# One inversion for both softmax sums, a gate product ahead of the fifth weight product, and later q/k loads, in an attention-plus-GLU kernel

## The chip, the cores and the metric

The kernel runs on one core of a Trainium2 chip. The metric is the device time of one execution in microseconds (us); an execution of this kernel takes about 829 us. The trace gives the *span*, from the first to the last instruction; it is some 1.7 to 2.2 us shorter than the time.

## The reference

For each of 4 batches (6016 rows, 256 columns) q and k are normalised by column and make a 256x256 matrix that passes through a softmax. v times that matrix goes into a gated unit.

```python
def _attn_ref(q, k, v, tau):
    qn = q / (np.linalg.norm(q, axis=1, keepdims=True) + 1e-06)
    kn = k / (np.linalg.norm(k, axis=1, keepdims=True) + 1e-06)
    s = kn.transpose(0, 2, 1) @ qn / tau
    s = s - s.max(-1, keepdims=True)
    a = np.exp(s)
    a /= a.sum(-1, keepdims=True) + 1e-09
    return (v @ a).astype(np.float32)

def _moe_ref(x, w_gate, w_val, w_out):
    gate = 1.0 / (1.0 + np.exp(-(x @ w_gate)))
    val = x @ w_val
    return (gate * val @ w_out).astype(np.float32)
```

## The kernel before

The kernel never forms v times the attention matrix. It multiplies the 256x256 matrix into the two weight matrices, G for the gate and H for the value (12 products per batch: three column groups, two matrices, two row halves), and then works on v directly. A *slot* is one step of the main loop: a gate pair of matmuls (`ps_gate`), a value pair (`ps_val`), the sigmoid on ScalarE, their product `hT` on VectorE, and four output matmuls (`ps_o`) of the chunk before. Twelve slots make a chunk of 512 rows. The next batch's loads, squares and scores are hung on slots as side work.

```python
def sums(b, i, pl=psm, tag="m"):          # one row half
    ps_r = pl.tile([P, 1], FP32, tag=tag, name="ps_r")
    for j in range(CB):
        mm(ps_r, s["e"][i][:, j, :], ones_bf[:, 0:1], j == 0, j == CB - 1)
    r = attp.tile([P, 1], FP32, tag=f"rrow{i}", name="rrow", bufs=2)
    invert(r, ps_r, 1e-9, 1.0)            # one add, one reciprocal on VectorE
# sums_both: the same for both halves in one PSUM tile, used by batches 1 to 3
# gh(b, n, pool, tag, act): product n into PSUM, then scaled by rrow and stored
# in bf16 by ScalarE (act) or VectorE
...
# batch 0, before the main loop
sums(0, 0)
gh(0, 0, psg, "g", act=False)
sums(0, 1, pss, "s")
gh(0, 1, psg, "g", act=True)
gh(0, 2, psv, "v", act=False)
gh(0, 3, psv, "v", act=True)
nc.scalar.preload_act_table(ACT.Sigmoid)
gh(0, 4, pso, "o", act=False)
...
# side work of batch b, for batch n = b + 1
at(ci * FC + 2, transpose_v, nb, nci)     # DMA transpose, SyncE's queue
at(ci * FC + 0, load_v, lb, lci)          # four v buffers, GpSimd's queue
first, last = (14 if b == 0 else 0), 8 * FC
for g, (t0, nt) in enumerate(groups):     # 12 groups of q and k
    s0 = first + g * (last - first) // NCH
    at(max(0, s0 - 20), load_qk, n, t0, nt)
...
# main loop
glu(b, ci, f)
flush()                                   # copies ps_o; the output store, SyncE's queue
if prev is not None and not block:
    out_mms(*prev, f * TPC, (f + 1) * TPC)
for fn, a in side.get((ci, f), ()):
    fn(*a)
if (b, ci) == (0, 0) and f < len(gh_order) - 5:
    gh(0, 5 + f, pso, "o")                # two PSUM tiles
```

## Time and profile before

| kernel before | value |
|---|---|
| median of three runs | 829.21 us (829.09, 829.21, 829.82) |
| the execution that the trace was taken in | 830.27 us, span 828.2 us |
| TensorE (PE) busy | 807.9 us, 98% |
| VectorE, ScalarE busy | 71%, 47% |

In this page PE is the bound; an idle PE costs its full length, and idleness elsewhere costs nothing. Useful here are PE's list of waits, the timeline with the time that an engine was idle before an instruction in square brackets, and the DMA issues with their time to landing. The traced execution was 1.06 us slower than the median.

### The profile page before, as it was taken

The numbers are of one execution on the slowest core, as the hardware profiler recorded it, in microseconds if no ns is written. First come the engines' busy times: TensorE is split into PE (matmuls) and PEld (weight loads), VectorE is DVE, ScalarE is ACT, GpSimd is POOL, SyncE is SP. The second block draws the span as 40 slices with busy tenths as digits, with TensorE's granted clock in tenths as the row PEclk, the third lists the DMA queues.
The fourth block names the chain that finished last, engine by engine and source line by source line (L and its number), as shares of the span: only waits on it lengthen the run. The fifth ranks groups of instructions, "written<-read, shape, count | busy, mean of one in ns | idle before, by whom it ended". The sixth has DMA issues, their size and how long they took to land.

```text
span 828.2 us, 13621 instructions
## 1 busy us (share of the span) xinstructions
PE 807.9 (98%) x5122; PEld 499.1 (60%) x5134; DVE 590.2 (71%) x1025; ACT 392.2 (47%) x644; POOL 78.9 (10%) x151
## 2 busy tenths in 40 slices
PE   4799999999999999999999999999999999999998
PEld 2456666665665666665576666666566566666666
DVE  5777777887667777778767777777766666666665
ACT  3754444446644444445654444444655444444442
POOL 4432100002201100000221010000000000000000
PEclk9999999999999999999999999999999999999999
DMA  9999823226746443223875452223322323322211
GB/s 214 206 200 195 126 52 89 55 58 133 158 85 124 96 85 60 57 51 83 157 141 123 81 108 60 51 60 78 64 58 63 75 52 84 61 58 68 47 36 71
DMA packets 77874, 77.17 MB, mean 93 GB/s; under 512 B 50672, under 2 KB 55792, under 8 KB 77808
## 3 DMA queue, kind: packets, MB, share of 16 engines
q0 software_dynamic: 22768, 38.81, 28.5%
q1 hardware_dynamic: 54752, 36.91, 17.6%
q8 instruction: 40, 0.66, 0.3%
q10 hardware_dynamic: 288, 0.59, 0.2%
q14 instruction: 26, 0.21, 0.1%
HBM read 78.64 MB, written 24.64 MB: 125 GB/s over the span
## 4 chain that ended last, share of the span: by engine, by line
PE 92%; DMA 6%; DVE 1%; issue 0%; POOL 0%; ACT 0%; POOLq 0%
PE ps_o L88 29%; PE ps_gate L88 29%; PE ps_val L88 29%; PE ps_s L88 4%; DMA k_sb<-in_k_dram 3%; PE ps_gh L88 2%; DMA vT<-v_sb 2%; DMA w_gate<-in_moe_w_gate_dram 1%; DVE hT L434 0%; DVE sq L184 0%; PE ps_end L88 0%; ACT g_sb L433 0%; POOL q_sb L98 0%; PE ps_n L88 0%; POOL k_sb L98 0%
## 5 line engine op out<-in xcount | busy, mean ns | idle before, releaser
L434 DVE TENSOR_TENSOR hT<-ps_val,g_sb 128x512 bf16<-128x512 f32 (+1 forms) x576 | 391.0, 679 | 205.7 <-ACT g_sb L433 200.8
L433 ACT ACTIVATE g_sb<-ps_gate 128x512 bf16<-128x512 f32 (+1 forms) x576 | 338.2, 588 | 386.8 <-PE ps_gate L88 380.5
L88 PE MATMUL ps_gate<-vT,gh_G 128*128 128x512 bf16 (+1 forms) x1152 | 337.5, 375 | 0.7 <-DMA vT<-v_sb 0.5
L88 PE MATMUL ps_val<-vT,gh_H 128*128 128x512 bf16 (+1 forms) x1152 | 337.5, 375 | 0.3
L88 PE MATMUL ps_o<-w_out_sb,hT 128*128 128x256 bf16 x2244 | 324.9, 273 | 0.0
L88 PEld LDWEIGHTS <-hT 128*128 128x128 bf16 x2268 | 221.0, 98 | 124.7
L88 PEld LDWEIGHTS <-gh_H 128*128 128x128 bf16 x1152 | 112.7, 98 | 131.7 <-issue 1.0
L88 PEld LDWEIGHTS <-gh_G 128*128 128x128 bf16 x1152 | 112.4, 98 | 38.3 <-DMA vT<-v_sb 0.8
L460 DVE COPY out_sb<-ps_o 128x256 f32<-128x256 f32 x187 | 77.4, 414 | 12.6 <-PE ps_o L88 12.6
L88 PE MATMUL ps_s<-k_sb,q_sb 128*128 128x256 bf16 x376 | 71.2, 293 | 14.6 <-DMA k_sb<-in_k_dram 7.6
L108 POOL DMA_DIRECT2D v_sb<-in_v_dram x48 | 25.5, 532 | 601.3 <-DMA vT<-v_sb 452.0
L88 PEld LDWEIGHTS <-q_sb 128*128 128x128 bf16 x376 | 39.2, 105 | 23.7 <-issue 9.6
L223 DVE TENSOR_TENSOR acc<-acc,sq 128x1024 bf16<-128x1024 bf16 (+1 forms) x66 | 44.2, 669 | 0.0
L184 DVE TENSOR_TENSOR sq<-q_sb 128x1024 bf16<-128x1024 bf16 (+2 forms) x42 | 28.0, 666 | 1.2 <-DMA q_sb<-in_q_dram 1.1
L98 POOL DMA_DIRECT2D q_sb<-in_q_dram x44 | 24.2, 549 | 38.5 <-PE ps_s L88 12.4
L98 POOL DMA_DIRECT2D k_sb<-in_k_dram x44 | 24.0, 544 | 14.5 <-DMA k_sb<-in_k_dram 7.7
L184 DVE TENSOR_TENSOR sq<-k_sb 128x1024 bf16<-128x1024 bf16 (+2 forms) x34 | 22.4, 658 | 0.2 <-DMA k_sb<-in_k_dram 0.2
L182 ACT ACTIVATE sq<-k_sb 128x1024 bf16<-128x1024 bf16 (+1 forms) x11 | 10.7, 1010 | 12.0 <-DMA k_sb<-in_k_dram 8.9
L88 PEld LDWEIGHTS <-e_sb 128*128 128x128 bf16 x112 | 10.2, 98 | 6.0 <-issue 1.0
L88 PE MATMUL ps_gh<-w_val,e_sb 128*128 128x512 bf16 x45 | 13.5, 379 | 0.2
L88 PE MATMUL ps_gh<-w_gate,e_sb 128*128 128x512 bf16 x41 | 12.7, 379 | 1.0 <-DMA w_gate<-in_moe_w_gate_dram 0.8
L433 ACT ACT_TABLE_LOAD x6 | 7.7, 1283 | 9.0 <-PE ps_gate L88 9.0
(69 smaller groups left out, 123.2 us busy)
## 6 DMA issues: line engine op xcount, KB each, us to landing
out_dram<-out_sb SPq DMA_DIRECT2D x44, 512.0 KB, 2.9
v_sb<-in_v_dram POOLq DMA_DIRECT2D x44, 256.0 KB, 3.9
q_sb<-in_q_dram POOLq DMA_DIRECT2D x35, 256.0 KB, 6.5
k_sb<-in_k_dram POOLq DMA_DIRECT2D x35, 256.0 KB, 7.7
q_sb<-in_q_dram POOLq DMA_DIRECT2D x4, 512.0 KB, 11.5
k_sb<-in_k_dram POOLq DMA_DIRECT2D x4, 512.0 KB, 13.4
out_dram<-out_sb SPq DMA_DIRECT2D x3, 384.0 KB, 3.0
w_gate<-in_moe_w_gate_dram POOLq DMA_DIRECT2D x3, 256.0 KB, 8.0
```

What stands on the lines that cost most here:

```text
L88: nc.tensor.matmul(out, lhsT=lhsT, rhs=rhs, start=start, stop=stop, **kw)
L98: nc.gpsimd.dma_start(out=tl[:, :nt, :], in_=rows(src, b)[:, t0 : t0 + nt, :])
L108: nc.gpsimd.dma_start(out=v_sb[:, :nt, :], in_=rows(v, b)[:, t0 : t0 + nt, :])
L182: nc.scalar.activation(out=sq[:, :nt, :], in_=src[:, :nt, :], func=ACT.Square)
L184: engine.tensor_tensor(out=sq[:, :nt, :], in0=src[:, :nt, :], in1=src[:, :nt, :], op=ALU.mult)
L223: nc.vector.tensor_tensor(out=acc[:, :nt, :], in0=acc[:, :nt, :], in1=st[b]["sq", w][:, :nt, :], op=ALU.add)
L433: nc.scalar.activation(out=g_sb[:, :n], in_=ps_gate[:, :n], func=ACT.Sigmoid)
L434: nc.vector.tensor_tensor(out=hts[b, ci][:, f, :n], in0=ps_val[:, :n], in1=g_sb[:, :n], op=ALU.mult)
L460: nc.vector.tensor_copy(out=out_sb[:, s, :], in_=ps)
```

## The change

Its intent: fewer VectorE steps between the sums and the first stores; the gate pair in place of a wait for weights; and q/k loads of the second batch that no longer crowd what is needed sooner.

```diff
-    sums(0, 0)
-    gh(0, 0, psg, "g", act=False)
-    sums(0, 1, pss, "s")
+    ps_first = gh_mms(0, 0, psg, "g")
+    sums_both(0)
+    gh_store(0, 0, ps_first, False)
     gh(0, 1, psg, "g", act=True)
     gh(0, 2, psv, "v", act=False)
     gh(0, 3, psv, "v", act=True)
     nc.scalar.preload_act_table(ACT.Sigmoid)
-    gh(0, 4, pso, "o", act=False)
...
-            half = nt * CB // 2
-            (nc.scalar.copy if late is None else late)(vT[:, half : nt * CB, :], ...)
+            half = nt * CB // 2 if late else nt * CB
+            if late:
+                late(vT[:, half : nt * CB, :], ...)
...
-            at(max(0, s0 - 20), load_qk, n, t0, nt)
+            at(max(0, s0 - (12 if b == 0 else 20)), load_qk, n, t0, nt)
...
+    gh_first = {f: (5 + f,) for f in range(len(gh_order) - 7)}
+    gh_first[len(gh_order) - 7] = tuple(range(len(gh_order) - 2, len(gh_order)))
...
-                glu(b, ci, f)
+                glu(b, ci, f, (lambda: gh(0, 4, pso, "o", act=False)) if first else None)
...
-                if (b, ci) == (0, 0) and f < len(gh_order) - 5:
-                    gh(0, 5 + f, pso, "o")
+                if (b, ci) == (0, 0):
+                    for i in gh_first.get(f, ()):
+                        gh(0, i, pso, "o")
```

`glu` calls its new argument between the gate pair and the value pair. The second transposed v tile now leaves PSUM through VectorE alone, and the last two products share slot 5.

More of the change, by code (lines that the diff above doesn't have):

```diff
@@ L336, in exps @@
         s.setdefault("rrow", [])
-    def sums(b, i, pl=psm, tag="m"):
-        s = st[b]
-        ps_r = pl.tile([P, 1], FP32, tag=tag, name="ps_r")
-        for j in range(CB):
-            mm(ps_r, s["e"][i][:, j, :], ones_bf[:, 0:1], j == 0, j == CB - 1)
-        r = attp.tile([P, 1], FP32, tag=f"rrow{i}", name="rrow", bufs=2)
-        invert(r, ps_r, 1e-9, 1.0)
-        s["rrow"].append(r)
     def sums_both(b):
@@ L370, with gh_mms @@
     gh_order = [(fg, w, i) for fg in range(NFG) for w in range(2) for i in range(CB)]
-    def gh(b, n, pl=None, tag=None, act=None):
+    def gh_mms(b, n, pl, tag):
         s = st[b]
         fg, w, i = gh_order[n]
-        ps = (pl or psm).tile([P, FG], FP32, tag=tag or "m", name="ps_gh")
+        ps = pl.tile([P, FG], FP32, tag=tag, name="ps_gh")
         for j in range(CB):
@@ L383, in gh, with gh_store @@
             )
+        return ps
+    def gh_store(b, n, ps, act):
+        s = st[b]
+        fg, w, i = gh_order[n]
         dst = s["gh"][w][fg][:, i, :]
         r = s["rrow"][i]
-        if act if act is not None else n % 2 == 0:
+        if act:
             nc.scalar.activation(out=dst, in_=ps, func=ACT.Copy, scale=r)
@@ L389, in gh @@
             nc.vector.tensor_scalar(out=dst, in0=ps, scalar1=r, scalar2=None, op0=ALU.mult)
+    def gh(b, n, pl, tag, act=None):
+        gh_store(b, n, gh_mms(b, n, pl, tag), n % 2 == 0 if act is None else act)
     vts = {}
@@ L406, in transpose_v @@
                 )
-            half = nt * CB // 2
-            (nc.scalar.copy if late is None else late)(vT[:, half : nt * CB, :], ps[:, half : nt * CB, :])
+            half = nt * CB // 2 if late else nt * CB
+            if late:
+                late(vT[:, half : nt * CB, :], ps[:, half : nt * CB, :])
             nc.vector.tensor_copy(out=vT[:, :half, :], in_=ps[:, :half, :])
@@ L412, with glu @@
     hts = {}
-    def glu(b, ci, f):
+    def glu(b, ci, f, between=None):
         t0, nt = groups[ci]
@@ L431, in glu @@
                 )
+            if between is not None and w is G:
+                between()
         g_sb = gpool.tile([P, CH], BF16, tag="g", name="g_sb")
@@ L602 @@
             for f in range(FC):
-                glu(b, ci, f)
+                first = (b, ci, f) == (0, 0, 0)
+                glu(b, ci, f, (lambda: gh(0, 4, pso, "o", act=False)) if first else None)
                 flush()
```

## The prediction

> **What bounds the kernel now.** I read four views of the kernel before: busy time by engine and in 40 slices, PE's waits, the timeline around the changed instructions, and the DMA queue's issues and landings. First the page:
>
> ```profile
> PE 807.9 (98%) x5122; PEld 499.1 (60%) x5134; DVE 590.2 (71%) x1025; ACT 392.2 (47%) x644; POOL 78.9 (10%) x151
> ...
> PE   4799999999999999999999999999999999999998
> ...
> PEclk9999999999999999999999999999999999999999
> DMA  9999823226746443223875452223322323322211
> ```
>
> PE (TensorE) is busy 807.9 of 828.2 us at full clock; only 20.3 us are idle in all, nearly all in the first two slices (some 41 us), where batch 0's q and k arrive and the attention matrix is made. Nothing in the diff touches the loads of that head or the number of large matmuls. So the change can only win pieces of idle PE time from about 35 us on. I looked for those. After 70 us PE's list of waits has a single entry:
>
> ```profile
> PE ps_gate L88 <- DMA vT<-v_sb: 0.5, 1, 0.5
> ```
>
> The rest lies in the start of the gate/value work. PE's timeline there, start first, then duration:
>
> ```profile
> 37.72 0.59 PE L88 MATMUL ps_gh<-w_val,e_sb 128*128 128x512 bf16 x2
> 37.95 0.69 ACT L387 ACTIVATE gh_G<-ps_gh,rrow 128x512 bf16<-128x512 f32 x1 [1.56 <-PE ps_gh L88]
> 38.57 0.59 PE L88 MATMUL ps_gh<-w_gate,e_sb 128*128 128x512 bf16 x2 [0.26 <-DMA w_gate<-in_moe_w_gate_dram]
> 39.00 0.59 PE L88 MATMUL ps_gate<-vT,gh_G 128*128 128x512 bf16 x2
> ...
> 42.53 0.59 PE L88 MATMUL ps_gh<-w_val,e_sb 128*128 128x512 bf16 x2
> 42.53 0.10 PEld L88 LDWEIGHTS <-e_sb 128*128 128x128 bf16 x1 [0.20 <-issue]
> ```
>
> A pair of 512-wide matmuls advances PE by 0.43 us (39.00 to 39.43; the 0.59 includes the tail). So PE was free at 37.72 + 0.43 = 38.15 and stood until 38.57 for the fifth G/H product, whose weight tile w_gate (second third) had only just landed. Weights come in the GpSimd queue's order: issued at 30.59, landing 7.94 later at 38.53. The second hole is the eighth product at 42.53: PE was ready at 42.02 + 0.43 = 42.45, so it costs 0.08.
>
> **What the Trainium skill says.** "TensorE: Matmul & The Clock Gate", Back-to-back issue gap, gives 518 cycles for a warm 512-column matmul, at 2.4 GHz 216 ns: the trace agrees (0.43 for two). "ScalarE: Activation LUTs", What ACT_TABLE_LOAD costs, has 1283 ns and a drain of about 1380 ns more. The trace has 1.28 us, and the sigmoid starts 1.29 us after the load starts (39.23 to 40.52), so I count 1.29 and no drain. "PSUM — Partial Sum Buffer", The four PSUM rules, says two sums in one bank work if only the first matmul carries the start flag and the columns are disjoint; the merged sum does so, as batches 1 to 3 already do. "DMA: Bandwidth & Descriptors", Queues, rings and completion order, says each DMA engine goes round between its queues packet by packet; so a transpose on SyncE's queue is slowed by loads on GpSimd's. The trace agrees: transposes land in 3.7 us at the median, but the one at 72.62 took 15.0.
>
> **The change, part by part.**
>
> *(1) One inversion.* It removes one add and one reciprocal of 128x1 on VectorE (0.15 + 0.17 us). But the sums now stand behind the first G/H product, which waits for its own weights until 36.19. Four sum matmuls then start at 36.63, cost about 0.03 us each (gap of 0.06 for two before), and their result reaches VectorE at about 36.95. Inversion takes two steps of 0.2, so the first G store starts at 37.35 (before: 36.84, since its sum had been inverted by 36.1) and ends at 38.1. ScalarE's G store starts at 37.38 instead of 37.95, because VectorE no longer does a 0.66 us store between the two inversions; it ends at 38.07 instead of 38.64. So both halves of G are ready 0.5 us sooner, at 38.1.
>
> *(2) Fifth product behind the first gate product.* The gate pair can thus start at 38.2 rather than 39.00, in the hole; the fifth product follows at 38.63, its weights landed, and the value pair at 39.06 rather than 39.43. H is just ready: VectorE stores at 38.0 to 38.75, ScalarE's store waits for the fourth product's end at 38.31 and runs 38.35 to 39.04. Gain here: 0.37 us.
>
> But this can't all be kept. ScalarE's sigmoid table load follows its H store: 39.05 against 39.23. The first sigmoid is then at 40.34 (before 40.52), and the VectorE work behind it (first hidden tile, then the store of the sixth product) moves by the same 0.18. The eighth product needs the PSUM buffer that this store frees: 42.35 instead of 42.53, with PE waiting from 42.08. So 0.37 shrinks to 0.18.
>
> *(3) Products eleven and twelve both in slot 5.* Before, the twelfth came in slot 6 and its VectorE store at 48.86 ended just too late for the ninth value pair, a loss of 0.02 us (the next start came 0.45 rather than 0.43 later). Now it needs the buffer of the tenth product one slot sooner. That store started at 46.27; moved by 0.18 it runs 46.09 to 46.83, while PE arrives at 46.66. Wait: 0.20 us. So 0.18 + 0.02 - 0.20: about nothing remains of parts 1 to 3.
>
> *(4) Second transposed v tile.* VectorE now copies all 128x1024 out of PSUM, ScalarE none. For 512 columns the two took 0.42 and 0.58 us. Doubling the streamed part I estimate 0.7 us on VectorE. It falls at 50.95 to 51.65 between two hidden tiles; the value pair at 52.49 needs the ninth-slot tile out of PSUM by then, and it is done at about 52.3. Hidden, with 0.2 us to spare.
>
> *(5) Loads eight slots later.* GpSimd runs ahead of the slots as far as buffers allow, so a slot number only sets the order in its queue. What matters is the order of q/k group 9 and v tile 7. Before, group 9 (slot 55) was ahead of v 7 (slot 60); now it is at 63, behind it. The views of GpSimd and SyncE around this:
>
> ```profile
> 68.84 0.53 POOL L98 DMA_DIRECT2D k_sb<-in_k_dram  x1 [0.68 <-DVE sq L184]
> 74.63 0.53 POOL L98 DMA_DIRECT2D q_sb<-in_q_dram  x1 [5.26 <-DVE hT L434]
> 75.15 0.54 POOL L98 DMA_DIRECT2D k_sb<-in_k_dram  x1
> 88.12 0.53 POOL L108 DMA_DIRECT2D v_sb<-in_v_dram  x1 [12.44 <-DVE hT L434]
> ...
> 72.62 2.08 SPq L401 DMA_TRANSPOSE vT<-v_sb  x1
> ...
> 86.52 0.60 PE L88 MATMUL ps_o<-w_out_sb,hT 128*128 128x256 bf16 x4
> 87.64 0.60 PE L88 MATMUL ps_gate<-vT,gh_G 128*128 128x512 bf16 x2 [0.52 <-DMA vT<-v_sb]
> ```
>
> v 7 needs the buffer of v 3, so it waits for the transpose of v 3, issued at 72.62 and landed at 87.6. Group 9's two loads go out at 74.63 and 75.15 and land 11.8 and 12.5 us later, at 86.4 and 87.65: they share the engines with the transpose to its very end. Behind v 7 they can't be issued until the transpose has landed. Left beside it is only the backlog up to group 8, whose k lands at 68.84 + 11.8 = 80.6. Two loads of 256 KB at the 210 GB/s of the saturated stretch are 2.5 us; 87.6 - 2.5 = 85.1 as a cautious estimate, 80.6 + 3.7 = 84.3 if the transpose gets through after the backlog. Either is ahead of 86.95, when PE wants it (86.52 + 0.43). PE then saves 87.64 - 86.95 = 0.69 us, all kept: the waits show nothing later that could absorb it.
>
> Sum: 0 from the head, 0.69 from the transpose, 829.21 - 0.69 = 828.5 us.
>
> **The rivals.** *A: the head's gain survives.* If the buffer waits at products eight and twelve are shorter than I reckon, up to 0.37 more is kept: 828.1 to 828.3. For it: 0.1 us decides each wait. Against: the ScalarE table load sits on the chain and moves only 0.18. *B: the transpose stays late,* because it is slow by itself or because the backlog drains later: then 829.0 to 829.3. For it: it runs in the densest DMA stretch, and the transpose at 44.94 took 16.1 us. Against: that one lay wholly within saturation, and this one has 14.3 us. *C: a new collision.* Groups 9 and 10 and v 7 now go out together at about 85, some 6 us of transfer, before the next transpose at 90.4, which took 8.6 us and is wanted some 14 us after its issue. It should still fit; if not, up to 1 us is lost, 829.3 or more. *D: VectorE becomes the bound at the double copy,* up to 0.3 us: 828.8.
>
> **Range and chances.** All of this is below 0.1% of the time, and three runs of before spread over 0.73 us. I say 828.5, with 827.9 (A on top and a good draw) to 829.2 (B, or head losses) 8 times in 10. A change of 2% would be 16.6 us, nearly all the idle time PE has; faster by that 0.01, slower 0.01, same 0.98.
>
> **What would show it.** In the changed trace: the first gate pair at about 38.2 with the fifth product behind it; value pair at 39.06; the sigmoid table load near 39.05; PE waits near 42.35 and 46.86; no wait for the transposed v near 87, the transpose landing by 85.1, and group 9's loads after it. The wait list after 70 us should then be empty of DMA. Wrong would be: a DMA wait that remains near 87 or appears near 104, or a gate pair still starting at 39.

## The result, and the profile after

| | median us | executions, us | mean us |
|---|---|---|---|
| before | 829.15 | 829.01, 829.08, 829.09, 829.21, 829.73, 829.82 | 829.32 |
| changed | 829.25 | 829.11, 829.13, 829.22, 829.29, 829.37, 829.46 | 829.26 |

The ratio is 0.9999, 95% interval 0.9986 to 1.0012: the same. A ratio here is the mean time of one kernel's fast runs over that of the other's of the same rounds, so not quite the ratio of the medians above. The trace of the changed kernel has a span of 827.4 us, 0.8 us under the 828.2 of before, in an execution of 829.46 us. Which execution each trace shows is thus the first question. PE's waits after 70 us are now an empty list. The head of the changed kernel (start, duration; a pair of 512-wide matmuls takes 0.43 of PE, and the rest of the 0.59 is its tail):

```profile
36.33 0.59 PE L88 MATMUL ps_gh<-w_gate,e_sb 128*128 128x512 bf16 x2 [1.18 <-DMA w_gate<-in_moe_w_gate_dram]
...
38.24 0.60 PE L88 MATMUL ps_gate<-vT,gh_G 128*128 128x512 bf16 x2
38.69 0.59 PE L88 MATMUL ps_gh<-w_gate,e_sb 128*128 128x512 bf16 x2
39.06 1.28 ACT L545 ACT_TABLE_LOAD   x1
39.12 0.59 PE L88 MATMUL ps_val<-vT,gh_H 128*128 128x512 bf16 x2
...
42.22 0.59 PE L88 MATMUL ps_gh<-w_val,e_sb 128*128 128x512 bf16 x2
...
46.10 1.24 PE L88 MATMUL ps_gh<-w_val,e_sb 128*128 128x512 bf16 x4
47.18 0.59 PE L88 MATMUL ps_gate<-vT,gh_G 128*128 128x512 bf16 x2
```

The gate pair sits where the hole was, and the fifth product comes after it. Four matmuls in a row without a wait take 1.02 us (the four w_val matmuls, two products, at 37.30 in the same trace); those at 46.10 take 1.24: the last product waits 0.22 us, and the experiment with four PSUM tiles below shows that it is for its PSUM tile. And the GpSimd, SyncE and PE lines around the transpose of v tile 3, and the landing of that transpose (the line "DMA to landing", in us from issue):

```profile
68.69 0.53 POOL L98 DMA_DIRECT2D k_sb<-in_k_dram  x1 [0.68 <-DVE sq L184]
81.17 0.53 POOL L108 DMA_DIRECT2D v_sb<-in_v_dram  x1 [11.95 <-DVE out_sb L462]
81.69 0.54 POOL L98 DMA_DIRECT2D q_sb<-in_q_dram  x1
82.20 0.55 POOL L98 DMA_DIRECT2D k_sb<-in_k_dram  x1
...
72.50 2.12 SPq L400 DMA_TRANSPOSE vT<-v_sb  x1
...
DMA to landing us min/median/max: 8.1/8.1/8.1
...
86.41 0.60 PE L88 MATMUL ps_o<-w_out_sb,hT 128*128 128x256 bf16 x4
86.84 0.59 PE L88 MATMUL ps_gate<-vT,gh_G 128*128 128x512 bf16 x2
```

v tile 7 goes out at 81.17, group 9's q and k only after it. The transpose lands 8.1 us after its issue, at 80.6, and PE's gate pair follows at 86.84 without a gap.

### The profile page after: what moved, and what is told of

Same layout as the page of the kernel before. It is cut to its first block, busy times and chain, and to the rows that moved or that the text cites. A ratio compares the mean times of both kernels' runs of the same rounds, so it can differ in the third digit from the quotient of the medians.

```text
span 827.4 us, 13618 instructions
## 1 busy us (share of the span) xinstructions
PE 806.2 (97%) x5122; PEld 498.6 (60%) x5134; DVE 590.3 (71%) x1023; ACT 392.0 (47%) x643; POOL 79.0 (10%) x151
## 4 chain that ended last, share of the span: by engine, by line
PE 94%; DMA 4%; DVE 1%; issue 0%; ACT 0%; POOL 0%; ACTq 0%; POOLq 0%
PE ps_o L88 30%; PE ps_val L88 29%; PE ps_gate L88 29%; PE ps_s L88 4%; DMA k_sb<-in_k_dram 3%; PE ps_gh L88 2%; DMA w_gate<-in_moe_w_gate_dram 1%; DVE hT L436 0%; ACT g_sb L435 0%; DVE sq L184 0%; PE ps_end L88 0%; PE ps_n L88 0%; DVE gh_G L385 0%; POOL q_sb L98 0%; PE ps_tp L403 0%
## 5 line engine op out<-in xcount | busy, mean ns | idle before, releaser
L88 PE MATMUL ps_s<-k_sb,q_sb 128*128 128x256 bf16 x376 | 70.1, 289 | 15.9 <-DMA k_sb<-in_k_dram 8.5
L435 ACT ACT_TABLE_LOAD x6 | 7.7, 1283 | 9.0 <-PE ps_gate L88 9.0
```

What stands on the lines that cost most here:

```text
L88: nc.tensor.matmul(out, lhsT=lhsT, rhs=rhs, start=start, stop=stop, **kw)
L435: nc.scalar.activation(out=g_sb[:, :n], in_=ps_gate[:, :n], func=ACT.Sigmoid)
```

## The experiments

Twelve kernels ran, in three batches of four, each batch on one chip beside the kernel before, five rounds each; all were correct. Every execution has its span, which is the finest measure. The expectations below count products from 0, so their "product seven" and "eleven" are the eighth and twelfth of the prediction.

### The two kernels again

No edit. The question is whether the trace of before shows a typical execution.

> The kernel before, unchanged. Theory A (the trace of before was taken in an execution of 830.27 us, 1.1 us over the median, so its 0.69 us wait for the transposed v tile is not in a typical execution): most executions have a span near 827.1 and 829.1 us, a few are 0.6 to 1.1 us longer, and a trace of a typical one shows no wait of PE near 87 us. Theory B (the wait is in every execution, and what the change won it lost to a lower granted clock, 0.996 against 1.000): every trace shows the wait near 87 us, the clock is 1.000, and the span is near 828.2 whatever the time. Ratio to itself 1.000 within 0.001.

> The changed kernel again. Theory A: 829.1 to 829.4 us, equal to the typical executions of before, with little spread because the wait cannot occur. Theory B: span 0.8 us below that of before in the same rounds, clock again 0.996 to 0.998. No wait for the transposed v tile in either.

On this chip (number 10) the kernel before fell into two kinds of execution, the changed one into a single kind:

| kernel, chip 10 | spans of its executions, us | mean time |
|---|---|---|
| before (beside all four) | 827.1, 827.2, 827.3, 827.4, 827.4 and 827.9, 828.0, 828.1, 828.4 | 829.56 |
| before, again | 827.1 and 828.1, 828.1, 828.1, 828.1 | 829.81 |
| changed, again | 827.1, 827.1, 827.2, 827.2, 827.2 | 829.12 |

Ratios to before: 1.0002 (0.9990 to 1.0015) and 0.9994 (0.9982 to 1.0007), both within noise. I had expected most executions of before to be short and a few long; on this chip eight of 14 were long. Here the median of before, again was 829.99 us and that of the changed kernel 829.13, so on this chip about as much as predicted was won, though the intervals do not separate it. The trace of before was this time taken in an execution of 829.03 us. PE's lines at the place where the first trace had its wait, the SyncE line with its landing, and the GpSimd lines:

```profile
86.14 0.60 PE L88 MATMUL ps_o<-w_out_sb,hT 128*128 128x256 bf16 x4
86.57 0.59 PE L88 MATMUL ps_gate<-vT,gh_G 128*128 128x512 bf16 x2
...
72.23 2.05 SPq L401 DMA_TRANSPOSE vT<-v_sb  x1
...
DMA to landing us min/median/max: 12.3/12.3/12.3
...
74.24 0.53 POOL L98 DMA_DIRECT2D q_sb<-in_q_dram  x1 [5.18 <-DVE hT L434]
74.76 0.54 POOL L98 DMA_DIRECT2D k_sb<-in_k_dram  x1
85.05 0.53 POOL L108 DMA_DIRECT2D v_sb<-in_v_dram  x1 [9.75 <-DVE out_sb L460]
```

Same kernel, same order of loads, no wait: the transpose took 12.3 us and landed at 84.5, 2 us before PE asked. In the first trace it had taken 15.0:

```profile
DMA to landing us min/median/max: 15.0/15.0/15.0
```

From 78 to 82 us the DMA engines moved 180 to 185 GB/s in this trace and 80 to 111 in the first, with no smaller share of busy time; why is not known. The clock theory falls: before had 1.000 in this trace and 0.994 to 0.998 in the others, long or short, and the changed kernel 0.997 to 0.998.

### Each half of the change alone

Head alone, the changed kernel with the loads put back:

```diff
-            at(max(0, s0 - (12 if b == 0 else 20)), load_qk, n, t0, nt)
+            at(max(0, s0 - 20), load_qk, n, t0, nt)
```

> The changed kernel with the loads back where they were (lead of 20 slots): head part alone. My sum: 0.1 to 0.2 us faster than before in the head, transpose of v tile 3 landing near 87 again with a wait of up to 0.7 us. Theory A: the wait comes and goes, so the median equals before within 0.2 us. Theory B: 0.7 us slower than the changed kernel in every execution.

Spans 827.2, 827.2, 827.2, 827.4 and one of 828.2; median 829.31, ratio 0.9999. The transpose took 14.2 us in its trace, with no wait. One long execution is still there. In the head I had expected 0.1 to 0.2 us; it was 0.05 against this chip's trace of before (13.44 against 13.49, table below).

Loads alone, the kernel before with the reverse edit:

> The kernel before with only the loads eight slots later. Transpose of v tile 3 lands near 80.6 as in the changed kernel, no wait near 87. Theory A: median within 0.2 us of before, executions above 829.6 gone. Theory B: 0.7 us below before in every execution, 0.1 us above the changed kernel.

Spans 827.3 to 827.4, none longer; median 829.24, ratio 0.9996. The transpose took 8.2 us. On this chip the later loads, here and in the changed kernel, had no long execution in ten, and the old order nine in 19: it is the order of the loads that goes with the long executions. A 0.2 us difference to the changed kernel is within what the landing of the first weights does: over the traces, the first product starts between 35.97 and 36.39 us.

### One group moved, or the transpose moved

If the cause is group 9's two loads beside the transpose, moving only that group should do, and so should moving only the transpose.

```diff
-            at(max(0, s0 - 20), load_qk, n, t0, nt)
+            at(61 if (b, g) == (0, 9) else max(0, s0 - 20), load_qk, n, t0, nt)
```

> The kernel before with one thing moved: only q/k group 9 goes behind v tile 7 in the GpSimd queue. Theory A (the slow executions of before, span 827.9 to 828.4 against 827.1 to 827.4, are those in which group 9's two loads hold the transpose of v tile 3 past the moment PE wants it): transpose lands near 81, no execution above 829.6, spans 827.1 to 827.4, like the changed kernel. Theory C (the slow executions come from the load phase of the first 36 us or from the granted clock): they stay, a third to a half of the runs near 830.

```diff
-                at(ci * FC + 2, transpose_v, nb, nci)
+                at(ci * FC + (-1 if (b, ci) == (0, 2) else 2), transpose_v, nb, nci)
```

> The kernel before with its loads where they were, but the transpose of v tile 3 ahead of the first output store in SyncE's queue, so it no longer waits until 72 us to be issued. Theory A: it is issued before 60 us, lands before 80, and the slow executions vanish though no load has moved: all spans 827.1 to 827.4. Theory C: the slow executions stay.

Group 9 alone brought the transpose to 8.6 us (landing at 80.8), as the whole shift does. The transpose moved ahead of the store was issued at 59.08 and took 16.1 us beside saturated loads, still landing at 75. Medians 829.20 and 829.15, spans 827.1 to 827.4 in both. But as a test of the long executions both were inconclusive: this chip (number 4) showed none in nine executions of before either, 827.1 to 827.5. A cause that comes and goes by chip can't be tested by taking it away where it is absent.

### Making the wait happen on a chip without it, and removing it again

A spare load of 256 KB right behind group 9, in the kernel before:

```diff
+            if (b, g) == (0, 9):
+                at(56, load_spare)      # 256 KB of q into a tile that nothing reads
```

> The kernel before with a spare load of 256 KB right behind group 9 in the GpSimd queue, more traffic beside the transpose of v tile 3. Theory A: the transpose lands 1 to 2.5 us later than in before (12.3 us in a fast, 15.0 in a slow execution), so PE waits in every execution: spans 828.0 to 829.5, none at 827.1. Theory C: a load more at 75 us changes nothing, half the spans stay at 827.1 to 827.4.

It ran on chip 4 with the two above: spans 828.3, 828.7, 828.8, 829.0, and one of 827.0; median 830.44, ratio 1.0012 (0.9999 to 1.0024). PE's waits and lines in the 829.0 execution:

```profile
PE ps_gate L88 <- DMA vT<-v_sb: 1.4, 1, 1.4
...
86.40 0.60 PE L88 MATMUL ps_o<-w_out_sb,hT 128*128 128x256 bf16 x4
88.42 0.60 PE L88 MATMUL ps_gate<-vT,gh_G 128*128 128x512 bf16 x2 [1.43 <-DMA vT<-v_sb]
```

PE lost 88.42 - 86.83 = 1.59 us, with the transpose at 15.9 us. One more load beside the transpose makes a chip without long executions have them in four of five. "In every execution", as I had written, was too strong: one escaped. Then the same traffic with each remedy: the transpose ahead of the store, and the loads eight slots later with the spare one still behind group 9 (slot 64):

> The kernel with the spare load (which made PE wait for the transposed v tile in 4 of 5 executions, spans 828.3 to 829.0), and the transpose of v tile 3 now ahead of the first output store. Theory A (all of the slow executions' time is PE's wait for that transpose): the transpose has landed by 77 us, the wait is gone and every span is 827.0 to 827.5 though the traffic is the same. Theory D (the extra traffic costs time in another way as well): spans stay above 827.9 in some executions.

> The kernel with the spare load, and the q/k loads eight slots later as in the change, the spare load still right behind group 9. Theory A: group 9 and the spare load both stand behind v tile 7 and so behind the transpose, which lands near 80.6; every span 827.0 to 827.5. If it is only the number of bytes in flight from 36 to 90 us that matters, spans stay at 828.3 to 829.0.

Chip 15: spans 827.1, 827.4, 827.4, 827.4, 827.6 with the transpose ahead, 827.1, 827.3, 827.4, 827.4, 827.6 with the loads later (medians 829.40 and 829.44); before beside them had 827.2 to 827.7 and one of 828.0. Both 827.6 are those of the lowest granted clock, 0.993; I expected at most 827.5. With the spare load still there, neither trace has a wait for a transposed tile: the transposes landed at 75.8 and 80.3. What is missing is the spare load without a remedy on this same chip: it ran on chip 4 only. So that the long executions went because of the remedies is not shown by these two counts; chip 15 might have had few of them anyway. The landing is firmer: with group 9 behind v tile 7 and the transpose in its old place, it took 8.1 to 8.6 us in every trace, on three chips. Under the later loads GpSimd's lines are:

```profile
80.83 0.53 POOL L112 DMA_DIRECT2D v_sb<-in_v_dram  x1 [11.95 <-DVE out_sb L464]
81.35 0.54 POOL L98 DMA_DIRECT2D q_sb<-in_q_dram  x1
81.87 0.55 POOL L98 DMA_DIRECT2D k_sb<-in_k_dram  x1
82.39 0.56 POOL L107 DMA_DIRECT2D spare<-in_q_dram  x1
```

v tile 7, which must wait for the transpose, stands guard ahead of them. The bytes are the same as in the kernel with the spare load on chip 4, where the transpose took 15.9 us; here it took 8.1. Their place behind that wait is what sets the landing.

### Where the head's gain went

The head's products 4 to 11 over four PSUM tiles in place of two (two of them are idle until slots 8 and 14):

```diff
+    head_ps = ((pso, "o"), (pso, "o"), (psm, "m"), (pss, "s"))
...
-                        gh(0, i, pso, "o")
+                        gh(0, i, *head_ps[i % 4])
```

> The changed kernel with products 4 to 11 going round four PSUM tiles (two as before, and the two that are idle until slots 8 and 14) instead of two. If the head's 0.37 us are lost to the PSUM buffer waits of products seven and eleven (my sum: 0.25 and 0.20), PE's starts in slots 0 to 8 close up: second transposed v tile 0.3 to 0.45 us earlier after the first product than the 13.44 us of the changed kernel, span 826.7 to 826.9, time 828.75 to 828.85. Rival: ScalarE's table load and the VectorE stores hold PE by other waits, and less than 0.1 us is gained.

And the changed kernel with one product per slot again (`gh_first = {f: (5 + f,) for f in range(len(gh_order) - 5)}`):

> The changed kernel with product eleven back in slot 6 (one per slot). My sum says that doubling up in slot 5 costs 0.20 us of waiting for the PSUM buffer and saves 0.02: so the second transposed v tile should come 13.25 us after the first product instead of 13.44, span 0.2 us shorter (826.9 to 827.2). Rival: the later store of product eleven holds the ninth value pair by as much as was won, 13.40 or more.

A ruler that is free of load jitter is the time from the start of the first product to the start of the second transposed v tile on PE (slot 8). All of the head's waits lie in it.

| kernel | first product | second v tile | between, us |
|---|---|---|---|
| before, first trace | 36.19 | 49.88 | 13.69 |
| before, second trace | 36.01 | 49.50 | 13.49 |
| loads alone | 36.22 | 49.75 | 13.53 |
| group 9 moved / transpose moved / more load | 36.02 / 36.25 / 36.23 | 49.50 / 49.74 / 49.76 | 13.48 / 13.49 / 13.53 |
| more load, loads later | 35.97 | 49.45 | 13.48 |
| more load, transpose ahead | 36.08 | 49.73 | 13.65 |
| changed / again / head alone | 36.33 / 36.08 / 36.14 | 49.77 / 49.52 / 49.58 | 13.44 |
| changed, one product per slot | 36.37 | 49.61 | 13.24 |
| changed, four PSUM tiles | 36.39 | 49.55 | 13.16 |

From there to the start of the last output products (`ps_end`) the distance is 772.92 to 772.93 us in every trace that has no wait for v, 773.62 in the first trace of before and 774.52 in that with the spare load. So the start of the first product, the head and that one wait account for all differences between these traces. One product per slot gives 0.20 us, as I had summed; medians were 829.11 (spans 827.0 to 827.3, chip 15). Four PSUM tiles give 0.28 us, just under the 0.3 to 0.45 that I expected, because the wait at the eighth product was only 0.06 and not 0.25; the median, 829.04 (spans 826.9 to 827.2, chip 4), missed its range too. The four tiles remove the wait of the doubled slot, seen in PE's lines of that run:

```profile
46.10 1.03 PE L88 MATMUL ps_gh<-w_val,e_sb 128*128 128x512 bf16 x4
46.96 0.59 PE L88 MATMUL ps_gate<-vT,gh_G 128*128 128x512 bf16 x2
```

### The best version

Four PSUM tiles and the transpose ahead of the store, on top of the change:

> Best version from these findings: four PSUM tiles for the head's products (0.28 us in the trace) and the transpose of v tile 3 ahead of the first store. Nothing more is expected from the second, as the loads are already out of its way: span 826.9 to 827.2, 828.85 to 829.1 us, no execution above 829.3.

Spans 826.9, 826.9, 826.9, 826.9, 827.2; median 828.98 against 829.45 for before beside it (chip 15), ratio 0.9994, interval 0.9981 to 1.0007. By medians it is the fastest of that batch, but at under 0.1% it is not a difference that the interval separates. The head took 13.17 us.

## Why the prediction was right or wrong

**Same, within 2%: right,** and easily so, whatever became of the mechanism: what the change could reach was 13.69 - 13.16 = 0.53 us in the head and 0.70 at the transpose, against 16.6 for 2%. The time itself was not met: 828.5 us was forecast and 829.25 came, just above the 827.9 to 829.2 that was given 8 chances in 10.

**The loads' mechanism: right.** Group 9's loads go behind v tile 7, so behind the transpose; the transpose lands before PE wants it; nothing new is awaited later, and the next transpose takes no longer (4.7 us, against 8.6 and 5.4 in the two traces of before). Only the landing was off: I had 84.3 to 85.1, and it was 80.6. I let the transpose begin its 3.7 us after the backlog, but the two drained together: group 8's k landed at 79.7, the transpose 0.9 us later.

**The step that failed** is the term "87.64 - 86.95 = 0.69 us, all kept", and before it the silent assumption that a trace's wait is in every execution. It measured 0.70 in the one trace (773.62 against 772.92) and 0 in the other; in the first rounds the median went from 829.15 to 829.25. On chip 10, nine of 19 executions with the old load order (before, before again, head alone) had spans of 827.9 or more; with the later loads, none of ten. On chip 4 none of nine of before had one, on chip 15 one of nine. Over all chips, no execution of a kernel with group 9 or the transpose out of the way reached 827.9, in 51 of them (the bound of 827.9 was set after chip 10 had been seen). A wait of 0.7 us that is in some executions moves a median only if it is in more than half of them, and in the first rounds it was in about two of six (829.73 and 829.82). I could have known: the trace was of an execution of 830.27 us, the median 829.21.

What is shown is this: the wait is there in one traced long execution and absent in a traced short one; more traffic beside the transpose brings long executions on chip 4, with the wait in the traced one; and on chip 10 the later loads had no long execution. That the transpose moved ahead removes them is not shown on a chip that had them. That each of the other long executions has the same wait is inferred from the counts and from the size, 0.5 to 1.3 us over the short ones' 827.1 to 827.4; the size is not matched closely, and part of it may be load jitter of the head. What stays open is why the same transfers take 12.3 us in one execution and 15.0 in another, and why some chips show it more.

**The head: right as a sum.** I had 0.37 won and all but nothing kept. Gate pair at 38.2 (38.24), sigmoid's table load at 39.05 (39.06), value pair at 39.06 (39.12), 0.20 us of waiting in the doubled slot (0.22) all came. The wait at the eighth product was too big in my sum, as told above. Kept were 0.04 to 0.09 us against the 13.48 to 13.53 of six traces with before's head. Two others had 13.65 and 13.69, and there it is 0.21 to 0.25. The first trace of before is one of these two and would again have overstated the gain: there w_gate's second third landed at 38.53, and the fifth product started 2.38 us after the first (2.34 in the other, 1.94 to 2.22 in the six). The prediction takes 518 cycles for a 512-column matmul from the Trainium skill's section on back-to-back issue; the page gives this figure for an isolated matmul and a smaller one, about 131 ns, for a stream. Here the stream ran at 0.43 us for two, so the measurement bears the first out and not the second.

**Rivals.** A (head gain survives) held at most in those hundredths. B (the transpose stays late) did not happen. C (a new collision) and D (VectorE bound by the double copy) did not: the copy of 128x1024 took 0.68 us where I estimated 0.7, and no wait of PE followed it.

## What to carry to other kernels

Before a wait in a trace is counted as a gain, compare the time of the traced execution with the median of the runs: a wait in a slow execution may be absent in most, and then its removal narrows the spread more than it moves the median. On a queue that issues in order, a slot number only sets the order, so put a load that competes with something urgent behind one that must wait for the urgent thing. When work is pulled forward by tenths of a microsecond, follow it to the next buffer it needs; here two PSUM tiles gave back most of what the earlier start had won.

## What the Trainium skill lacked or had wrong

- "ScalarE: Activation LUTs", What ACT_TABLE_LOAD costs, adds about 1380 ns of drain to the 1283 ns of a table load. In these traces the sigmoid begins 1.29 us after the load begins in the kernel before and 1.30 in the changed one (39.06 to 40.36), and the load begins 0.02 and 0.01 us after the end of the store ahead of it: no separate drain was paid there.
- "DMA: Bandwidth & Descriptors", Queues, rings and completion order, says that the engines alternate between queues packet by packet, but gives no measure of how far that stretches a transpose. Here the median of all such transposes was 3.7 us. That of v tile 3 took 8.1 to 8.6 beside a backlog that drains, 12.3 to 15.0 with two loads more, 15.9 with three, and 15.2 to 16.2 wholly inside saturated traffic; and it differed by 2.7 us between two executions of one kernel.
- "Perfetto Trace Analysis" has no advice on whether the traced execution is a typical one. Here the first trace was of an execution of 830.27 us against a median of 829.21, and 0.69 us of its waits were not typical.
